# Attention and gated feed-forward on one core: the second tile's first weight columns put ahead of the first tile's second columns

## Chip, cores and metric

The kernel runs on one core of one Trainium2 chip. The metric is the device time of one execution in microseconds (us). The engines are TensorE (PE, with its weight loads PEld), VectorE (DVE), ScalarE (ACT), GpSimd (POOL) and SyncE (SP), which here issues most of the loads.

## What is computed

Causal attention with a decay for each head (no softmax), and after it a feed-forward block whose two up projections are multiplied with each other. All is in float32.

```python
def _attn_ref(q, k, v):                     # B, H, S, D = 8, 8, 576, 64
    scores = scale * np.matmul(q, k.transpose(0, 1, 3, 2))
    gamma = 1.0 - 2.0 ** (-5.0 - np.arange(H, dtype=np.float32))
    Dmat = np.where(rel >= 0, gamma[:, None, None] ** rel[None, :, :], 0.0)
    return np.matmul(scores * Dmat[None, :, :, :], v)

def _moe_ref(x, w1, w2, w3, w_out):         # x 4608x512, w1 and w2 512x1024, w3 1024x1024, w_out 1024x512
    a = x @ w1
    b = x @ w2
    h = a * b @ w3
    return h @ w_out
```

The weights arrive as float64; the kernel makes float32 of them from their bits.

## The kernel before

**Attention in units.** The batches are taken in four pairs, and the 576 positions of a pair in five chunks (64, then four of 128). A pair and a chunk make a unit; units 0 to 4 are the first pair. For a unit g, `load(g, ...)` issues the loads of k, q and v on SP's queue (L93). `scale(g, "q", True)` multiplies q by its decay on ACT, one instruction for each of eight heads (L202); `scale(g, "v", ...)` does the same for v. `front(g, names)` transposes k or q on PE into two PSUM banks (L218) and copies each bank to SBUF on ACT (L221). `score(g)` makes the score products on PE (L233) and multiplies them by the mask on DVE, four instructions (L236). `state(g)` adds k and v into the running state on PE (L255) and copies it on ACT (L259). `pv(g)` multiplies state and masked scores with q and v on PE (L274, L299); the function that it returns copies the result on ACT into the transposed tokens xT (L306).

**Tokens in tiles.** A pair has three tiles of 192 positions for each of its two batches, called (pair, n). Tile (0,0) is complete after unit 2, tile (0,1) after unit 3, and tile (0,2) after unit 4. `strassen_tokens(i, n, engine)` makes the four sums over a tile's quarters that the products need (L496).

**Up steps.** w1 and w2 are cut into four groups of 256 columns each. `up(i, n, fp, conv)` multiplies tile (i, n) with group fp of both weights by Strassen's scheme of seven products (Winograd's form), in a fixed order, each 8 matmuls (L528). `plus` adds a finished product on DVE to another part of the tile `c` (L533); it then runs `conv` steps of the weight conversion and one piece of work that was set aside in the list `aside`. Product p1 is copied to c by ACT twice (L546, L561), and at the end DVE multiplies the two halves of c into `ab` (L566). There is one buffer for c. Product S4 x B22, the last, is added onto the bank p5 after p5 has been read by the third `plus`.

**Weight conversion.** The weights come in blocks (0 to 3 make group 0, then four to a group), each loaded into one of five raw buffers (L342, L345). `conversion()` is a generator, and `convert(n)` runs n steps of it. To begin a block takes two steps: three ACT instructions for the exponents (L395 to L397; for block 7 L393 and L397) with DVE's L399, and DVE's L402. To end it takes two more: DVE's L413, and L426, which also calls for the next load. The exponents have two buffers. After the last block of a group three more steps make that group's weight sums S3, S2, and S1 with S4 (L149). `live["S", fp]` tells that they are issued; an up step needs them and calls for missing ones itself.

**Order.** The schedule is manual: each engine gets its instructions in the order in which the Python code issues them. From unit 3 on this order is written out by hand (L771 to L814): after `state(3)` the code converts until the sums of group 1 are issued, then come the scores of unit 3, the up step of tile (0,0) with group 1, the front of unit 4 (k and q), the output of unit 3, the token sums of tile (0,1), the scores of unit 4, the up step of tile (0,1) with group 0, the output of unit 4, and the up step of tile (0,1) with group 1. The number in `owed` is a count of conversion steps that the next up step runs after its first copy.

```python
def plus(ps, to, sb):
    nc.vector.tensor_add(c[:, to], ps, c[:, sb])
    convert(conv.pop(0) if isinstance(conv, list) else conv)
    for extra in (aside, spread):
        if extra:
            extra.pop(0)()
```

The first up step, `up(0, 0, 0, ..., first=True)`, has the list `aside` filled with: the scaling of q of unit 2 (run by the up step itself), an empty piece, the scaling of v of unit 2 on DVE, the front of k and the front of q of unit 2. Its `conv` is [0, 0, 2, 2, 2].

Of the kernel before, what the change touches and what calls it, by code (L numbers as in the profile page):

```python
# [19 lines left out]
def kernel(  # L20
# [13 lines left out]
    nc = tc.nc  # L34
# [160 lines left out]
    def scale(g, nm, scalar=False, engine=nc.gpsimd):  # L195
        c = g % NC
        sz = sizes[c]
        t, gam = live[nm, g], {"q": gq, "v": gk}[nm]
        t = t[:sz].rearrange("p (b h) d -> p b h d", b=2)
        if scalar:  # L200
            for h in range(H) if scalar is True else scalar:
                nc.scalar.mul(t[:, :, h, :], t[:, :, h, :], gam[:sz, c, h:h + 1])  # L202
            return
        engine.tensor_tensor(
            out=t, in0=t, in1=gam[:sz, c].unsqueeze(1).unsqueeze(3).to_broadcast([sz, 2, H, D]), op=ALU.mult)

    def front(g, names="kq"):
        c = g % NC
        sz = sizes[c]
        for nm in names:  # L210
            src = live[nm, g]
            dst = pools["fr"].tile([P, 2, NP, P], F32, tag=nm + "T", name=nm + "T",
                                   bufs=1 if nm == "k" and g >= NC else 2)
            for b in range(2):
                tp = acc.tile([P, NP, P], F32, tag="acc", name="tp")
                for p in range(NP):
                    h = b * H + 2 * p
                    nc.tensor.transpose(tp[:, p, :sz],  # L218
                                        src[:sz, h:h + 2, :].rearrange("p a d -> p (a d)"),
                                        ident[:sz, :sz])  # L220
                nc.scalar.copy(dst[:, b, :, :sz], tp[:, :, :sz])  # L221
            live[nm + "T", g] = dst

    def score(g):
        c = g % NC
        sz = sizes[c]
        kT, qT = live["kT", g], live["qT", g]
        pm = pools["fr"].tile([P, 2, 2, NP, P], F32, tag="pm", name="pm", bufs=1)
        for b in range(2):
            sc = [acc.tile([P, NP, P], F32, tag="acc", name="sc") for j in range(2)]  # L230
            for p in range(NP):
                for j, hs in enumerate(heads):
                    nc.tensor.matmul(sc[j][:sz, p, :sz], kT[hs, b, p, :sz], qT[hs, b, p, :sz],  # L233
                                     start=True, stop=True)
            for j in range(2):
                nc.vector.tensor_mul(pm[:sz, b, j, :, :sz], sc[j][:sz, :, :sz],  # L236
                                     mask[:sz, :sz].unsqueeze(1).to_broadcast([sz, NP, sz]))
        live["pm", g] = pm

    def state(g):  # L240
        c = g % NC
        sz = sizes[c]
        if c == NC - 1:
            return
        vs = live["v", g]
        kn = live["k", g]
        if c == 0:
            live["st"] = st_ps.tile([P, 2, NP, D], F32, tag="st", name="st")
        st = live["st"]

        for b in range(2):
            for p in range(NP):
                for j, hs in enumerate(heads):
                    h = b * H + 2 * p + j
                    nc.tensor.matmul(st[hs, b, p, :], kn[:sz, h, :], vs[:sz, h, :],  # L255
                                     start=(c == 0 and b == 0 and p == 0), stop=(c == NC - 2),
                                     skip_group_check=True)
        sb = pools["fr"].tile([P, 2, NP, D], F32, tag="sb", name="sb")
        nc.scalar.copy(sb, st)  # L259
        live["sb", g + 1] = sb  # L260
# [17 lines left out]
    def pv(g):  # L278

        if ("xps", g) not in live:  # L280
            pv_state(g)
        i, c = divmod(g, NC)
        sz = sizes[c]
        live["x", g] = True
        vs, pm, banks = live["v", g], live["pm", g], live["xps", g]

        parts = []
        for n in range(NB):
            lo, hi = max(starts[c], n * TB), min(starts[c] + sz, (n + 1) * TB)
            if lo < hi:  # L290
                m = i * NB + n
                if ("xT", m) not in live:
                    live["xT", m] = xps[m % 4 == 3].tile([P, NP, 2, TB], F32, tag="xT", name="xT")
                parts.append((live["xT", m], lo - n * TB, lo - starts[c], hi - lo))
        for m, (b, n) in enumerate(bank_order):
            for r in range(2):
                for half in range(2):
                    p, j = 2 * r + n, half ^ r
                    nc.tensor.matmul(banks[r][heads[half], b, n, :sz], vs[:sz, b * H + 2 * p + j, :],  # L299
                                     pm[:sz, b, j, p, :sz], start=(c == 0 and m == 0), stop=True,  # L300
                                     skip_group_check=True)

        def evict():
            for x, to, fr, n in parts:
                for r in range(2):
                    nc.scalar.copy(  # L306
                        x[:, 2 * r:2 * r + 2, :, to:to + n].rearrange("p n b s -> p b n s"),
                        banks[r][:, :, :, fr:fr + n])

        return evict  # L310
# [152 lines left out]
    def convert(n):  # L463

        for _ in range(n):
            if go_on() is not None:
                return
# [43 lines left out]
    def up(i, n, fp, conv=0, tail=True, first=False):  # L511
        m = every.index((i, n))
        while ("S", fp) not in live:
            assert go_on() is None
        if ("B", i, n) not in live:
            list(strassen_tokens(i, n))
        if fp == 0:
            live["ab", i, n] = (pools["ab3"] if m == 2 else ffn).tile([P, 2 * KF, TB], F32, tag="ab", name="ab")
        ab = live["ab", i, n]

        def product(ps, a, b):
            a, b = A(fp, a), live["B", i, n][b]
            new = ps is None
            if new:
                ps = acc.tile([P, 2, TB], F32, tag="acc", name="up")
            for w in range(2):
                for r in range(2):
                    nc.tensor.matmul(ps[:, w, :], a[:, w, r, :], b[:, r, :], start=(new and w == r == 0),  # L528
                                     stop=(w == r == 1), skip_group_check=True)
            return ps  # L530

        def plus(ps, to, sb):
            nc.vector.tensor_add(c[:, to], ps, c[:, sb])  # L533
            convert(conv.pop(0) if isinstance(conv, list) else conv)
            for extra in (aside, spread):
                if extra:
                    extra.pop(0)()


        sums = ()  # L540
        if fp == NQ - 1 and m < NB - 1 and has_x(*every[m + 1]) and ("B", *every[m + 1]) not in live:
            sums = strassen_tokens(*every[m + 1], nc.vector, True)
            aside.extend([lambda: next(sums)] * 4)
        c = ffn.tile([P, 4, 2, TB], F32, tag="c", name="c", bufs=1)
        p1 = product(None, "A11", "B11")
        nc.scalar.copy(c[:, 0], p1)  # L546

        convert(owed.pop() if owed else 0)
        if first:

            p7 = product(None, "S3", "T3")
            product(p1, "A12", "B21")
            aside.pop(0)()
        plus(product(None, "S2", "T2"), 1, 0)
        plus(p7 if first else product(None, "S3", "T3"), 2, 1)
        p5 = product(None, "S1", "T1")
        plus(p5, 3, 2)
        plus(product(None, "A22", "-T4"), 2, 2)
        if not first:
            product(p1, "A12", "B21")  # L560
        nc.scalar.copy(c[:, 0], p1)  # L561
        product(p5, "S4", "B22")
        plus(p5, 1, 1)

        list(sums)
        nc.vector.tensor_mul(ab[:, 4 * fp:4 * fp + 4, :], c[:, :, 0, :], c[:, :, 1, :])  # L566
        if tail:
            convert(conv)
# [224 lines left out]
    copies()  # L793
    load(4, "v")
    state(3)
    while ("S", 1) not in live:
        convert(1)
    score(3)
    aside.append(lambda: scale(4, "q", True))
    up(0, 0, 1, conv=2, tail=False)  # L800
    owed.append(2)
    front(4)
    convert(1)
    pv(3)()
    list(strassen_tokens(0, 1, nc.vector))
    score(4)
    aside.append(lambda: scale(4, "v", True))
    up(0, 1, 0, conv=2, tail=False)
    owed.append(2)
    pv(4)()  # L810
    up(0, 1, 1, conv=[2, 1, 0, 2, 2], tail=False)
    owed.append(2)
    up(0, 0, 2, conv=[2, 1, 1, 2, 2], tail=False)
# [509 lines left out]
```

## Time and profile before

| | us |
|---|---|
| median of 3 runs (lowest to highest) | 831.22 (830.67 to 832.04) |
| the profiled execution | 832.77 |
| its span, first to last instruction | 831.0 |
| granted TensorE clock, mean | 0.999 |

Where the first 100 us go on PE, ACT and DVE (busy us in each stretch of 10 us):

| stretch | PE | DVE | ACT | DMA share |
|---|---|---|---|---|
| 30 to 40 | 9.03 | 8.84 | 7.67 | 1.07 |
| 40 to 50 | 9.41 | 9.66 | 8.72 | 0.99 |
| 50 to 60 | 8.59 | 9.35 | 8.53 | 1.09 |
| 60 to 70 | 9.96 | 8.40 | 7.14 | 0.94 |
| 70 to 80 | 9.53 | 9.79 | 7.52 | 0.20 |
| 80 to 90 | 10.00 | 9.29 | 6.02 | 0.38 |

A row tells how long an engine was at work in that stretch; 10 means all the time. The change lies between 35 and 93 us. In a line of the timeline the first two figures are start and length in us, then come engine, line, operation and operands, the count of merged instructions, and in brackets the engine's idle time before it with what ended it.

### The profile page before, as it was taken

How to read it: one execution, taken by the hardware profiler on the slowest of the kernel's cores; microseconds unless marked ns; L12 is line 12 of the kernel's file. 1: busy time of each engine (PE TensorE's matmuls, PEld its weight loads, DVE VectorE, ACT ScalarE, POOL GpSimd, SP SyncE). 2: the span in 40 equal slices, each digit the busy share in tenths (PEclk: the TensorE clock that was granted, in tenths of full speed). 3: DMA queues.
4: the chain of work that ended last, by engine and by line, in shares of the span. 5: the costliest groups of instructions: out<-in, count | busy, mean ns of one | idle time of the engine just before them, and what ended most of it. 6: DMA issues, size and time to landing. Idle time of an engine off the chain costs nothing.

```text
span 831.0 us, 15815 instructions
## 1 busy us (share of the span) xinstructions
PE 817.5 (98%) x6117; PEld 737.0 (89%) x6117; DVE 547.6 (66%) x962; ACT 291.8 (35%) x609; POOL 222.3 (27%) x258
## 2 busy tenths in 40 slices
PE   8999999999999999999999999999999999999998
PEld 8889999744888998889999889998889998899987
DVE  4899999993544568754657755677745667646653
ACT  4787556572021111255443024341034331033300
POOL 1000000001303332125547015565006460045600
PEclk9999999999999999999999999999999999999999
DMA  9995454446237665988786347978245453146401
GB/s 191 226 224 137 79 131 134 117 126 104 99 66 195 113 151 186 266 264 206 200 228 184 92 88 209 240 224 217 56 92 180 163 191 114 36 149 214 141 26 51
DMA packets 196812, 126.96 MB, mean 153 GB/s; under 512 B 157848, under 2 KB 178456, under 8 KB 196736
## 3 DMA queue, kind: packets, MB, share of 16 engines
q1 hardware_dynamic: 168560, 50.40, 29.6%
q0 software_dynamic: 12480, 65.67, 24.3%
q10 hardware_dynamic: 15696, 9.87, 4.5%
q8 instruction: 48, 0.79, 0.4%
q14 instruction: 28, 0.23, 0.1%
HBM read 103.62 MB, written 22.28 MB: 152 GB/s over the span
## 4 chain that ended last, share of the span: by engine, by line
PE 89%; DVE 6%; DMA 2%; issue 1%; SPq 1%; ACT 1%; ACTq 0%; POOL 0%; DVEq 0%; POOLq 0%
PE po L651 24%; PE up L1060 17%; PE up L528 14%; PE seed L1060 13%; PE ps L477 7%; PE xps L299 3%; PE sc L233 3%; PE xps L274 2%; PE tp L218 2%; PE st L255 1%; SPq L171 1%; DVE pm L236 1%; DVE ab L1032 1%; PE idle L131 1%; DMA ld_v<-in_v_dram 1%
## 5 line engine op out<-in xcount | busy, mean ns | idle before, releaser
L651 PE MATMUL po<-w3o,ab 128*128 128x256 f32 x552 | 125.0, 381 | 2.3 <-DVE ot L655 1.0
L651 PEld LDWEIGHTS po<-w3o,ab 128*128 128x128 f32 x552 | 103.7, 190 | 18.9 <-DVE ot L655 2.5
L1065 POOL TENSOR_TENSOR cc<-cc 128x384 f32<-128x384 f32 x112 | 109.3, 1002 | 3.8 <-ACT cc L1083 2.4
L1072 DVE TENSOR_TENSOR cc<-seed,cc 128x384 f32<-128x384 f32 x88 | 48.7, 553 | 69.0 <-PE seed L1060 59.3
L181 POOL TENSOR_TENSOR bl_q<-bl_q,gqs 128x512 f32<-128x512 f32 (+1 forms) x26 | 26.0, 1020 | 185.8 <-DMA bl_q<-in_q_dram 182.3
L1060 PE MATMUL up<-xT,ra 128*128 128x192 f32 x384 | 73.7, 328 | 0.1
L528 PE MATMUL up<-xT,wA 128*128 128x192 f32 x384 | 70.7, 328 | 1.0 <-DVE xT L496 1.0
L236 DVE TENSOR_TENSOR pm<-sc,mask 128x512 f32<-128x512 f32 (+1 forms) x80 | 45.4, 627 | 35.1 <-PE sc L233 35.1
L1072 DVE TENSOR_TENSOR cc<-up,cc 128x384 f32<-128x384 f32 x88 | 48.5, 551 | 30.2 <-PE up L1060 21.8
L533 DVE TENSOR_TENSOR c<-up,c 128x384 f32<-128x384 f32 x80 | 44.1, 552 | 36.7 <-PE up L528 35.7
L651 PE MATMUL po<-wB,forms 128*128 128x256 f32 x288 | 65.4, 379 | 0.7 <-DVE pm L236 0.7
L528 PEld LDWEIGHTS up<-xT,wA 128*128 128x128 f32 x384 | 63.3, 190 | 2.4 <-PE up L528 1.2
L1060 PEld LDWEIGHTS up<-xT,ra 128*128 128x128 f32 x384 | 63.7, 190 | 1.4 <-DMA ra<-kept 0.4
L961 POOL DMA_DIRECT2D ra<-kept x54 | 30.5, 565 | 118.7 <-PE seed L1060 93.8
L651 PEld LDWEIGHTS po<-wB,forms 128*128 128x128 f32 x288 | 54.6, 190 | 8.4 <-DVE pm L236 1.1
L1079 ACT COPY seed<-up 128x384 f32<-128x384 f32 x56 | 25.9, 463 | 100.2 <-PE up L1060 56.6
L477 PE MATMUL ps<-wo,w3T 128*128 128x512 f32 x128 | 55.1, 592 | 0.0
L1060 PE MATMUL up<-ra 128*128 128x192 f32 x288 | 54.7, 326 | 0.0
L477 PEld LDWEIGHTS ps<-wo,w3T 128*128 128x128 f32 x128 | 24.3, 190 | 30.1 <-issue 29.7
L1060 PE MATMUL seed<-e,ra 128*128 128x192 f32 x256 | 50.9, 329 | 0.0
L1060 PEld LDWEIGHTS up<-ra 128*128 128x128 f32 x288 | 48.1, 190 | 0.1
L528 PE MATMUL up<-T,wS 128*128 128x192 f32 x256 | 46.7, 326 | 1.4 <-DVE wS L149 1.4
(134 smaller groups left out, 1479.1 us busy)
## 6 DMA issues: line engine op xcount, KB each, us to landing
ra<-kept POOLq DMA_DIRECT2D x54, 896.0 KB, 4.9
raw<-in_moe_w_dram SPq DMA_DIRECT2D x72, 128.0 KB, 3.0
bl_q<-in_q_dram SPq DMA_DIRECT2D x192, 32.0 KB, 3.3
out_dram<-ot ACTq DMA_DIRECT2D x41, 128.0 KB, 2.3
bl_k<-in_k_dram SPq DMA_DIRECT2D x136, 32.0 KB, 3.5
raw<-in_moe_w_dram SPq DMA_DIRECT2D x16, 256.0 KB, 5.4
ld_k<-in_k_dram SPq DMA_DIRECT2D x8, 512.0 KB, 6.1
raw<-in_moe_w_out_dram SPq DMA_DIRECT2D x32, 128.0 KB, 2.8
```

What stands on the lines that cost most here:

```text
L181: nc.gpsimd.tensor_tensor(out=part, in0=part, in1=gqs[:, :, n0:n0 + n].unsqueeze(3).to_broadcast([P, NP, n, BL]), op=ALU.mult)
L233: nc.tensor.matmul(sc[j][:sz, p, :sz], kT[hs, b, p, :sz], qT[hs, b, p, :sz], start=True, stop=True)
L236: nc.vector.tensor_mul(pm[:sz, b, j, :, :sz], sc[j][:sz, :, :sz], mask[:sz, :sz].unsqueeze(1).to_broadcast([sz, NP, sz]))
L477: nc.tensor.matmul(ps, live["w3T", ft][:, g, :], live["wo"][:, g, :], start=(g == 0), stop=(g == KF - 1))
L528: nc.tensor.matmul(ps[:, w, :], a[:, w, r, :], b[:, r, :], start=(new and w == r == 0), stop=(w == r == 1), skip_group_check=True)
L533: nc.vector.tensor_add(c[:, to], ps, c[:, sb])
L651: nc.tensor.matmul(ps[nm], a[A][:, f, :], live["W"][B][:, f, :], start=(f == 0 and not on), stop=(f == NP - 1), skip_group_check=True)
L961: engine.dma_start(ring[n % 3], kept[n % 14 // 7][nm])
L1060: nc.tensor.matmul(ps[:, w, :], weight_of(slot, a, w), B[b], start=(new and w == 0), stop=True, skip_group_check=True)
L1065: nc.gpsimd.tensor_tensor(out=o, in0=o, in1=i, op=ALU.add)
L1072: nc.vector.tensor_add(c[:, j], ps, with_add[:, j])
L1079: nc.scalar.copy(p6, p1)
```

## The change

Two things are edited. In the first up step, `plus` runs the piece of set-aside work before the conversion steps and not after them; other up steps are as they were. And the hand-written order after `state(3)` becomes: scores of unit 3; scaling of q and front of k of unit 4; output of unit 3; token sums of tile (0,1); front of q of unit 4; one conversion step; scores of unit 4; the up step of tile (0,1) with group 0, with three conversion steps in each `plus` in place of two; output of unit 4; conversion until the sums of group 1 are issued; the up step of tile (0,0) with group 1; the up step of tile (0,1) with group 1 as before. The scaling of q of unit 4 is issued directly, and no longer as a set-aside piece of an up step.

```diff
         def plus(ps, to, sb):
             nc.vector.tensor_add(c[:, to], ps, c[:, sb])
+            if first and aside:
+                aside.pop(0)()
             convert(conv.pop(0) if isinstance(conv, list) else conv)
-            for extra in (aside, spread):
+            for extra in (spread,) if first else (aside, spread):
                 if extra:
                     extra.pop(0)()
...
     state(3)
+    score(3)
+    scale(4, "q", True)
+    front(4, "k")
+    pv(3)()
+    list(strassen_tokens(0, 1, nc.vector))
+    front(4, "q")
+    convert(1)
+    score(4)
+    aside.append(lambda: scale(4, "v", True))
+    up(0, 1, 0, conv=3, tail=False)
+    pv(4)()
     while ("S", 1) not in live:
         convert(1)
-    score(3)
-    aside.append(lambda: scale(4, "q", True))
     up(0, 0, 1, conv=2, tail=False)
     owed.append(2)
-    front(4)
-    convert(1)
-    pv(3)()
-    list(strassen_tokens(0, 1, nc.vector))
-    score(4)
-    aside.append(lambda: scale(4, "v", True))
-    up(0, 1, 0, conv=2, tail=False)
-    owed.append(2)
-    pv(4)()
     up(0, 1, 1, conv=[2, 1, 0, 2, 2], tail=False)
     owed.append(2)
```

## Prediction

> **What bounds the kernel now.** I read the page first, then busy time by stretches, then who TensorE (PE) waited for, then the timeline around the change, then the landing times of the loads in it.
>
> ```profile
> PE 817.5 (98%) x6117; PEld 737.0 (89%) x6117; DVE 547.6 (66%) x962; ACT 291.8 (35%) x609; POOL 222.3 (27%) x258
> ```
>
> The whole-kernel shares say TensorE. By stretches (length, busy PE, PEld, DVE, ACT, POOL, clock, DMA share, GB/s):
>
> ```profile
> 49.70:92.70 43.00, 41.04 (x409) 39.00 (x410) 38.97 (x69) 30.48 (x60) 0.00 (x0) 1.00 0.63 149
> 92.70:157.00 64.30, 64.27 (x392) 63.36 (x392) 61.93 (x110) 38.89 (x59) 0.00 (x0) 1.00 0.52 123
> 157.00:212.50 55.50, 55.50 (x134) 24.89 (x133) 35.15 (x53) 26.27 (x38) 4.01 (x4) 1.00 0.50 109
> ```
>
> The moved steps lie in the first row. PE idles 1.96 us there, which is all that a better order can win. From 92.70 PE has no hole, so a delay handed on there stays to the end. VectorE (DVE) is busy 62 of 64 us: it has no room either. The holes by cause (us, times, longest):
>
> ```profile
> PE up L528 <- DVE wS L149: 1.4, 1, 1.4
> ...
> PE st L255 <- DVE ld_v L204: 0.6, 1, 0.6
> PE up L528 <- DVE c L533: 0.5, 1, 0.5
> ```
>
> The 1.4 is the first tile's second up step waiting for weight sums, at 55.79. Around it (start, length, engine, line):
>
> ```profile
> 45.83 5.16 SPq L93 DMA_DIRECT2D ld_q<-in_q_dram  x1
> ...
> 50.82 2.06 PE L233 MATMUL sc<-qT,kT 64*128 64x128 f32 x32
> ...
> 51.72 0.69 DVE L402 SCALAR_TENSOR_TENSOR m<-raw,m 128x512 f32<-128x512 uint32 x1
> ...
> 55.79 1.54 PE L528 MATMUL up<-T,wS 128*128 128x192 f32 x8 [1.41 <-DVE wS L149]
> ...
> 56.88 2.48 DVE L236 TENSOR_TENSOR pm<-sc,mask 128x512 f32<-128x512 f32 x4
> 56.98 2.43 ACT L202 ACTIVATE ld_q<-ld_q,gq 128x128 f32<-128x128 f32 x8
> ```
>
> The first line is the load of the fifth unit's q. Its landing (last figure, us from issue):
>
> ```profile
> ld_q<-in_q_dram SPq DMA_DIRECT2D x1, 512.0 KB, 10.9
> ```
>
> So it lands at 45.83 + 10.9 = 56.7, and its scaling by ScalarE (ACT) ran from 56.98. The same front end later:
>
> ```profile
> 67.88 1.10 ACT L221 COPY qT<-tp 128x512 f32<-128x512 f32 x2
> 68.54 2.06 PE L233 MATMUL sc<-qT,kT 64*128 64x128 f32 x32
> 68.83 1.24 ACT L306 COPY xT<-xps 128x256 f32<-128x256 f32 x4
> 69.55 0.56 DVE L496 TENSOR_TENSOR xT<-xT 128x384 f32<-128x384 f32 x1 [0.94 <-ACT xT L306]
> ...
> 70.52 1.57 PE L528 MATMUL up<-xT,wA 128*128 128x192 f32 x8
> ```
>
> What follows calls units and weight blocks by their numbers, and writes up(t,f) for the up step of tile t of the first pair with weight group f; durations in sums are taken from start to start.
>
> **The change, part by part.** *(a) In the first up step, the set-aside work is issued ahead of the conversion steps.* No instruction is added. On ACT the kT copies of unit 2 (37.23, 1.07) pass block 4's exponents (35.02 to 37.31), the qT copies pass block 5's. kT cannot start before its transposes (36.59 plus about 0.6), so it keeps 37.23; block 4 takes block 5's slot (38.19), qT stays at 40.41, and block 5 (2.3) now stands ahead of the copy of c at L561: 43.7 instead of 41.35. The product at L566 needs that copy, so it goes from 42.94 to 44.15, and DVE behind it (mask products of unit 2, block 6, scaling of v3) shifts by 1.2; ACT likewise. PE follows by about 1.2 at the third unit's transposes. On the final time I price this at 0, because the wait in (b) covers it: with the shift, the mask products of unit 3 end at 56.1 and its output matmuls at about 58, still before the q that (b) waits for. Without that cover it costs 1.2.
>
> *(b) score(3), scaling of q4, front of unit 4, pv(3), token sums, score(4) come before up(0,1), which gives way to up(1,0).* Before, up(0,1), 7 products x 1.30 = 9.1 us of PE, hid the landing of q4, its scaling and the fronts. Now nothing does. ACT takes them as written: scaling 56.75 to 59.15 (2.43), kT copies to 60.2 (1.07), xT copies of pv(3) to 61.35 (1.24), qT copies from 61.3, the first half done at 61.85 (0.53). PE runs dry at about 58, does the q transposes as heads arrive, and starts score(4) at 61.9; 1.97 later, at 63.9, up(1,0) starts. In the trace of before the same work plus up(0,1) was done at 70.52. Loss: 63.9 + 9.15 - 70.52 = **+2.5**. The removed 1.41 and 0.6 are already inside this difference. Queued behind the waiting scaling on ACT: kT, xT, qT; behind xT on DVE: the token sums, block 7's end, the mask products. DVE ends L402 at 52.41 and the mask products of unit 3, now next, at 54.9 (2.48), or 56.1 with (a); then it stands still until the first two xT copies are done, at 60.85 (0.72 after their start, as at 68.83 and 69.55): 4.8 us of an engine that has no slack.
>
> *(c) up(1,0) with 3 conversion steps per sum instead of 2.* DVE: token sums 60.85 to 62.98 (2.13), L413 of block 7 (0.61), mask products to 66.0 (2.4), first sum at 66.8, when PE's second product ends. Then L426, S3, S2, S1, S4 (0.61+0.70+0.72+0.61+0.61), second sum (0.47), L399, L402 (1.05), third sum ends 72.6. PE's last product adds onto the bank that the third sum reads; it is ready at 63.9 + 7.91 = 71.8 and starts at 72.65. That 0.85 replaces the 0.47 at 79.06; from start to last product 8.75 against 8.54: **+0.2**. pv(4) follows with no wait, up(0,1) starts 4.43 later (79.06 to 83.49 in the trace): 77.1.
>
> *(d) up(0,1), now here.* The fifteenth step of (c) puts block 11's exponents (2.3) on ACT. They need one of two buffers, freed by block 9's L426 at 78.25, and end at 80.55; xT copies of unit 4 (1.08) and the copy at L546 (0.5) stand behind them, so c is ready at 82.05. DVE finished L566 at 79.45: another 2.6 idle. Sum 0.47, L402, L413 (1.2), sum 0.47, L426, L399 (1.05), third sum ends 85.8; PE is ready for its last product at 77.1 + 7.91 = 85.0. **+0.85**, and up(1,1) starts at 87.15 (83.49 before).
>
> *(e) up(1,1), unmoved.* DVE arrives late: fourth and fifth sums with L426, S3, S2, S1, S4 end at 91.1, L566 at 92, two owed steps 93.0, then sum, L413, L426, sum, L399, sum to 96.15; PE is ready at 95.05. **+1.1.** up(0,2) then starts at about 97.4 against 92.70, and its own third sum (100.1 + 4.5 = 104.4) is before PE's 105.3. One conversion step fewer in all (26 against 27 here) is caught up later and costs nothing: w3's third transposed tile is ready at 163.8 (L430, 162.59 + 1.25) and wanted at 171 (157.2 plus two tiles of 55.1/8). Loads: the SP queue gets the same transfers; those of blocks 12 to 15 come up to 11 us later, but with over 5 us before their exponents.
>
> **Sum:** 2.5 + 0.2 + 0.85 + 1.1 = +4.65. The profiled execution took 832.77, its span 831.0, with 1.8 outside the span; the sum makes it 837.4. Against the median of 831.22, which I use: **835.9**.
>
> **Unknown prices.** The landing: DMA was at its limit there, so the SP queue shifts little; 0.5 us earlier or later moves (b) by 0.5. The waits (c) to (e) come from adding some 40 DVE and ACT rows: between 0 (then +2.5 less the 0.47 that goes, 833.2) and 1.5 more than I have. (a) between 0 and 1.2.
>
> The clock in all rows above is 1.00, with no PE hole longer than 1.4; the new hole is some 3 us with eight transposes in it, and I price it at 0. The Trainium skill (TensorE: Matmul & The Clock Gate, Why this matters for your kernels) says that gaps over about 3 us between bursts bring the clock back to half, and Part 4 of it that transposes do not count as busy. By that, an estimate, a half-speed window of 3.4 us would add 1.7, and the time would be 837.6; no trace here shows such a gap.
>
> **Rivals.** *Overlap wins (faster).* up(1,0) needs no second columns, so PE works while DVE makes their sums, and the 1.41 + 0.47 go: 829.3. The place is score(4). It decides if up(1,0) starts 4.65 earlier than 63.9, at 59.2, thus q4 landing by 52.0, 6.2 after its issue; if (c) to (e) vanish with it, 54.2 is enough. The measured 10.9 and 2.43 speak against. 5%.
>
> *Only the hole at score(4).* DVE catches up in (c) to (e) because the sums are hidden by free banks: 833.2. For it: before, DVE recovered its lag by 86.47. Against: the third sum must be read before PE's last product, whatever banks are free. 22%.
>
> *More than the sum.* (a) isn't covered, 1.2, or the waits (c) to (e) are the full 1.5 larger, or both: 837.1 to 838.6. 10%.
>
> *Nothing changes.* A later stage takes the delay in, 831.2. Against: PE 64.27 of 64.30 and 55.50 of 55.50. 6%.
>
> **Numbers.** My forecast has 57%. Its own range is 834.3 to 837.2; the range to hold 8 in 10 goes down to the second rival and up past (a): 832.7 to 837.8. A change of 0.2% (1.7 us) is about what a measurement here can tell from none. Faster by that 0.05, within it 0.07 (nothing changes, and the low edge of the second rival), slower 0.88.
>
> **What will show it.** In the new trace: scaling of q4 on ACT at about 56.7 behind the DMA; score(4) at about 62, up(1,0) at 64; DVE idle before the token sums 4 to 6 us; a wait of the first sum of up(0,1) on ACT's L546; three waits of PE on c L533 near 1 us each; up(0,2) at 97.4; equal spacing after it. Score(4) before 60, or a PE without those three waits, would prove me wrong.

## The result, and the profile after

The changed kernel took 837.83 us in the median (835.52 to 840.66, 6 runs), the kernel before 831.34 (830.67 to 833.33, 6 runs). The ratio is 1.0075, 95% interval 1.0052 to 1.0098: slower by 6.5 us where 4.7 were forecast. The forecast was 835.9, with 832.7 to 837.8 as its range; the median lies at the upper end of it. The interval means 4.3 to 8.1 us more, so the times alone do not set the forecast's 4.7 apart from the 6.5. The profiled execution of the changed kernel took 839.02, its span 837.3 (before 832.77 and 831.0): 6.3 more in the spans, and these 6.3 are accounted for here.

The busy line of the page, after the change:

```profile
PE 820.6 (98%) x6117; PEld 738.5 (88%) x6117; DVE 548.2 (65%) x962; ACT 291.2 (35%) x609; POOL 222.0 (27%) x258
```

The share of TensorE is 98% as before: the loss doesn't show there. Busy time by stretches does show it (length, PE, PEld, DVE, ACT, POOL, clock, DMA share, GB/s). The first stretch holds the same work as 49.70 to 92.70 before, up to the start of up(0,2):

```profile
49.60:98.64 49.04, 43.79 (x412) 40.51 (x410) 39.24 (x69) 30.65 (x61) 0.00 (x0) 0.97 0.52 128
98.64:163.00 64.36, 64.33 (x393) 63.53 (x393) 61.96 (x111) 38.37 (x58) 0.00 (x0) 1.00 0.53 123
163.00:218.50 55.50, 55.50 (x134) 24.89 (x133) 35.94 (x55) 27.11 (x40) 3.78 (x4) 1.00 0.51 110
```

It is 6.04 longer (49.04 against 43.00), and up(0,2) starts 5.94 later, at 98.64 instead of 92.70. PE idles 5.25 us in it where it idled 1.96, and PE's own busy time grew by 2.75 though its work is the same: 1.6 of that is score(4) and the first product after it, the rest is nearly all in the transposes (L218, 2.94 instead of 1.91), which now run as the heads of q4 arrive. The clock column is new: 0.97 instead of 1.00. The next two stretches are as long as before, so nothing was given back.

Who PE waited for (us, times, longest), the two rows that grew:

```profile
PE up L528 <- DVE c L533: 2.3, 3, 0.9
PE sc L233 <- ACT qT L221: 2.0, 2, 1.8
```

The wait for weight sums is gone, 1.4 us. In its place stand 1.8 for the transposed q of unit 4 and three waits for sums of c. The chain that ended last (start, length, what) goes through the first of them:

```profile
45.56 10.81 DMA ld_q<-in_q_dram
56.39 2.45 ACT ld_q L202 x8
58.84 0.95 ACT kT L221 x2
59.79 1.08 ACT xT L306 x4
60.87 0.50 ACT qT L221
61.41 3.40 PE sc L233 x32
```

Load of q4, scaling, kT copies, xT copies, qT copies, score(4): the queue that the prediction wrote down, in its order. The timeline of the rows around it, with what each engine waited for in brackets:

```profile
60.35 0.56 DVE L496 TENSOR_TENSOR xT<-xT 128x384 f32<-128x384 f32 x1 [4.52 <-ACT xT L306]
...
61.41 3.40 PE L233 MATMUL sc<-qT,kT 64*128 64x128 f32 x32 [1.75 <-ACT qT L221]
...
64.74 1.81 PE L528 MATMUL up<-xT,wA 128*128 128x192 f32 x8
...
73.82 1.57 PE L528 MATMUL up<-xT,wS 128*128 128x192 f32 x8 [0.77 <-DVE c L533]
...
83.18 0.56 DVE L533 TENSOR_TENSOR c<-up,c 128x384 f32<-128x384 f32 x1 [2.37 <-ACT c L548]
...
86.98 1.57 PE L528 MATMUL up<-xT,wS 128*128 128x192 f32 x8 [0.66 <-DVE c L533]
...
97.23 1.57 PE L528 MATMUL up<-xT,wS 128*128 128x192 f32 x8 [0.89 <-DVE c L533]
...
98.64 1.46 PE L528 MATMUL up<-xT,wA 128*128 128x192 f32 x8
```

DVE stands still for 4.52 ahead of the token sums, and for 2.37 ahead of the first sum of up(0,1), behind ACT's copy (L546 before, two lines lower now). What the sum did not have is the length of score(4): 3.40 for 32 matmuls that took 2.06 before. The stretches of 2 us around it:

```profile
58.00:60.00 2.00, 1.32 (x8) 0.67 (x6) 0.00 (x0) 2.00 (x7) 0.00 (x0) 1.00 1.26 262
60.00:62.00 2.00, 0.59 (x8) 0.59 (x10) 1.58 (x3) 1.84 (x6) 0.00 (x0) 0.96 1.00 210
62.00:64.00 2.00, 2.00 (x24) 2.00 (x22) 2.00 (x5) 0.00 (x0) 0.00 (x0) 0.50 0.45 103
64.00:66.00 2.00, 2.00 (x14) 1.78 (x13) 1.58 (x3) 0.00 (x0) 0.00 (x0) 0.68 0.68 218
66.00:68.00 2.00, 2.00 (x14) 2.00 (x13) 0.16 (x2) 1.41 (x5) 0.00 (x0) 1.00 0.16 52
```

PE worked 1.9 of the 4 us ahead of 62. Then its clock was granted at 0.50, from about 61.9 to 65.3. Score(4) and the first product of up(1,0) ran in that time: 3.33 from start to start instead of 1.98, and 1.65 instead of 1.41, so 1.6 us.

### The profile page after: what moved, and what is told of

It reads as the page before. It is cut to its first block, busy times and chain, and to the rows that moved or that the text cites. A ratio compares the mean times of both kernels' runs of the same rounds, so it can differ in the third digit from the quotient of the medians.

```text
span 837.3 us, 15813 instructions
## 1 busy us (share of the span) xinstructions
PE 820.6 (98%) x6117; PEld 738.5 (88%) x6117; DVE 548.2 (65%) x962; ACT 291.2 (35%) x609; POOL 222.0 (27%) x258
## 4 chain that ended last, share of the span: by engine, by line
PE 82%; DVE 7%; DMA 4%; issue 3%; ACT 2%; SPq 1%; POOL 1%; ACTq 0%; DVEq 0%; POOLq 0%
PE po L653 24%; PE up L1062 16%; PE seed L1062 12%; PE up L528 12%; PE ps L477 7%; PE sc L233 3%; PE xps L299 3%; PE xps L274 1%; DMA ld_q<-in_q_dram 1%; PE st L255 1%; PE tp L218 1%; SPq L171 1%; DMA ra<-kept 1%; DVE ab L1034 1%; DVE c L533 1%
## 5 line engine op out<-in xcount | busy, mean ns | idle before, releaser
L653 PE MATMUL po<-w3o,ab 128*128 128x256 f32 x552 | 124.9, 381 | 2.3 <-DVE ot L657 1.0
L653 PEld LDWEIGHTS po<-w3o,ab 128*128 128x128 f32 x552 | 103.7, 190 | 18.8 <-DVE ot L657 2.5
L653 PE MATMUL po<-wB,forms 128*128 128x256 f32 x288 | 65.4, 379 | 0.3 <-DVE pm L236 0.3
L653 PEld LDWEIGHTS po<-wB,forms 128*128 128x128 f32 x288 | 54.6, 190 | 8.1 <-DVE pm L236 0.7
```

The lines of the kernel that those rows point to most:

```text
L653: nc.tensor.matmul(ps[nm], a[A][:, f, :], live["W"][B][:, f, :], start=(f == 0 and not on), stop=(f == NP - 1), skip_group_check=True)
```

## The experiments

My theory after the result: PE is held at score(4) by ACT's queue behind q4; the hole lets the clock fall; and DVE, stopped ahead of the token sums and again behind ACT's exponents, makes three later products wait. Rivals: the first edit is to blame; or the early landing of q4 alone would make the change win; or DVE's lateness is a matter of ACT's queue only. "1.0069 (1.0057 to 1.0081)" is a ratio to the kernel before on the same chip, with its 95% interval. The kernel before took 832.3 to 832.4 there.

**The changed kernel once more.**

> The changed kernel itself, beside the next three on one chip. Its loss against the kernel before should again be 0.5 to 1.0%, and its times should spread by several us, since the fall of the clock depends on where its 3.41 us windows lie: with the clock falling for one window, for two, or not at all.

839.51, ratio 1.0085 (1.0069 to 1.0101), 837.67 to 841.43. In the profiled execution score(4) took 3.78, and the clock stayed at 0.50 for two windows, 6.83 us, as expected of some executions: from the start of score(4) to the second product of up(1,0) it is 6.24 us, against 4.98 in the first profile and 3.39 before. The loss is there again.

**Filler matmuls in the hole.** `keep_busy(n)`, which the kernel has already, multiplies the identity n times with itself on PE; nobody reads the result.

```diff
     list(strassen_tokens(0, 1, nc.vector))
+    keep_busy(3)
     front(4, "q")
+    keep_busy(7)
     convert(1)
     score(4)
```

> The changed kernel with filler matmuls on PE: three ahead of the q transposes of unit 4 and seven behind them, so that PE has work while it waits for score(4). Theory (the clock fell to 0.50 from 61.9 to 65.3 because PE ran dry at 58): the clock stays at 1.00, score(4) takes 2.0 instead of 3.40 and the first product 1.55 instead of 1.81, the time falls by about 1.6 to 836.2, and the runs lie closer together. Rival (the clock is not moved by the idle time, or the lost time is hidden by DVE being late anyway): no change, 837.8.

```profile
59.55 1.73 PE L131 MATMUL idle<-ident 128*128 128x128 f32 x14
...
61.45 2.06 PE L233 MATMUL sc<-qT,kT 64*128 64x128 f32 x32 [0.18 <-ACT qT L221]
```

With PE kept at work the clock stayed at 1.00 (0.999 or 1.000 in the mean of all five executions), score(4) took 2.06, and up(1,0) started at 63.44 instead of 64.74. That the idle time moves the clock is shown. What it is worth in time isn't: 837.87, ratio 1.0069 (1.0057 to 1.0081), against 1.0075 and 1.0085 with overlapping intervals, where 836.2 was expected. Its five times lie within 1.9 us, those of the changed kernel within 5.1 and 3.8; since the kernel before itself spread by 2.9 over the 11 runs beside this one and by 4.0 over 18 others, this proves little. In the profile up(0,2) starts 1.53 earlier than in the changed kernel, but 0.9 of that is lost after it, in waits of PE for DVE at L653 and L1064 that are longer in this execution by about 1; whether that is chance is open.

**The new order without the first edit.** (`plus` as before the change.)

```diff
-            if first and aside:
-                aside.pop(0)()
             convert(conv.pop(0) if isinstance(conv, list) else conv)
-            for extra in (spread,) if first else (aside, spread):
+            for extra in (aside, spread):
```

> The changed kernel without its first edit: the first up step converts ahead of the set-aside work, as before. Theory (the 1.2 us by which that edit delays DVE is covered by the wait for q4 on ACT): mask products of unit 3 end about 1.2 earlier, score(4) starts within 0.3 of 61.4, the time stays at 837.8 within 0.7. Rival (the first edit's delay is handed on): 836.6, and score(4) starts near 60.2.

838.43, ratio 1.0075 (1.0061 to 1.0089). The mask products of unit 3 start at 52.15 instead of 53.36, as expected 1.2 earlier, and score(4) starts at 61.66. The first edit costs nothing in the new order, since the wait for q4 covers it. The rival that blames it falls.

**The first edit alone, on the kernel before.** (The same two lines, put in.)

> The kernel before with the first edit alone (set-aside work ahead of the conversion steps in the first up step). Theory (without the wait for q4 that covers it, its delay of DVE by 1.2 reaches PE, since the second up step waits for weight sums that DVE makes in order): the wait of 1.41 at 55.79 grows to about 2.6, the time to 832.5. Rival (it is hidden on PE): 831.3.

```profile
55.60 1.54 PE L528 MATMUL up<-T,wS 128*128 128x192 f32 x8 [1.41 <-DVE wS L149]
```

833.19 against 832.42, ratio 1.0005 (0.9992 to 1.0017): between 0.7 us gained and 1.4 lost, which holds both theories. The profile says more. From score(2) to the second product of up(0,1) it is 15.87 us (39.73 to 55.60), before 14.76 (41.03 to 55.79): the delay of 1.1 is there and reaches PE. It doesn't come as a longer wait for the weight sums, as I had expected; that stays at 1.41, because PE itself is late, after waits for mask products (0.44, before none) and for v3 (0.85, before 0.59). In this execution the opening was 1.3 earlier, which hides it in the span.

**Block 11's exponents after the first copy of up(0,1).**

```diff
-    up(0, 1, 0, conv=3, tail=False)
+    up(0, 1, 0, conv=[3, 3, 3, 3, 2], tail=False)
+    owed.append(1)
     pv(4)()
```

> The changed kernel, with the last conversion step of up(1,0) (it begins block 11) run after the first copy of up(0,1) instead. Theory (block 11's exponents on ACT stand ahead of the copy at L548, which the next sum of DVE waits for): that copy moves from 82.66 to about 80.5, DVE's wait of 2.37 there goes nearly to 0, PE's waits for c in up(0,1) and up(1,1), 0.66 and 0.89, go to below 0.3 each, the time falls by about 1.3 to 836.5. Rival (DVE is late from its stop ahead of the token sums, whatever ACT does): the waits stay, 837.8.

```profile
81.32 0.48 ACT L548 COPY c<-up 128x384 f32<-128x384 f32 x1 [0.26 <-DVE ab L568]
...
82.11 0.56 DVE L533 TENSOR_TENSOR c<-up,c 128x384 f32<-128x384 f32 x1 [0.54 <-PE up L528]
```

The copy now waits for `ab` and no longer for the exponents, and DVE's 2.37 became 0.54, spent on PE. PE's last products in up(0,1) and up(1,1) show no wait; the one in up(1,0), 0.77, stays. 837.22, ratio 1.0051 (1.0037 to 1.0065), against 1.0075 and 1.0085 of the changed kernel: 0.24 to 0.34% less, where 0.16% was expected, though the clock was low for 6.83 us in its profile. So ACT's three instructions did cause two of the three waits.

**Four conversion steps in DVE's stop.**

```diff
     pv(3)()
+    convert(4)
     list(strassen_tokens(0, 1, nc.vector))
     front(4, "q")
-    convert(1)
     score(4)
     aside.append(lambda: scale(4, "v", True))
-    up(0, 1, 0, conv=3, tail=False)
+    up(0, 1, 0, conv=[3, 3, 2, 2, 2], tail=False)
```

> The changed kernel with four conversion steps (the end of block 7 and the sums of group 1, 3.3 us of DVE) ahead of the token sums of tile (0,1), where DVE stands still for 4.5 us, and fewer in up(1,0), the same in all. Theory (DVE's stop ahead of the token sums is what makes its sums late later): PE's waits for c in up(1,0), up(0,1) and up(1,1), 0.77, 0.66 and 0.89, go to below 0.2 each; 2.2 less than the changed kernel; score(4) still starts at 61.4 and the clock still falls. Rival (only the ACT exponents of block 11 matter, as e4 moved them): the first wait stays, at most 1.5 less.

All of PE's waits in this stretch, 49 to 100 us:

```profile
PE sc L233 <- ACT qT L221: 1.8, 1, 1.8
PE st L255 <- DVE ld_v L204: 0.8, 1, 0.8
PE tp L218 <- ACT ld_q L202: 0.5, 2, 0.3
```

All three waits for c are gone, the first too. Score(4) starts at 61.37 and takes 3.66. 835.71, ratio 1.0047 (1.0030 to 1.0064), against 839.51 of the changed kernel on the same chip: 3.8 less, 2.2 were expected. A part of the 3.8 is the clock's: among executions with the same mean clock, 0.998, it is 835.59 and 835.78 against 837.67 and 838.52, 2.4 less. Block 11's exponents come earlier by themselves, at 76.20 instead of 79.51, because DVE frees their buffer earlier (L426 at 75.26 instead of 78.78), and no longer hold up the copy of c. So the lateness of DVE explains all three waits; moving ACT's exponents was another way to give a part of it back.

The length of the stop is not what counts. In the runs that keep ACT's order and leave the conversion behind the stop, DVE's idle time ahead of the token sums goes from 3.98 us (the load of q4 first, below) to 6.34 (the changed kernel once more), and the first wait for c is 0.77 in all of them. What counts is the 3.3 us of conversion that come after the stop and not in it.

**The same, with the filler matmuls.** (Both edits.)

> As the second kernel of this group, with the filler matmuls of the first experiment. Theory (clock and DVE's lateness are separate terms): no fall of the clock, score(4) in 2.06, 1.5 less than the second kernel in the middle and a narrower spread, leaving the wait of score(4) itself, +2 to +2.5 against the kernel before. Rival (filling does not pay, as the first experiment's time, 837.87, seems to say): the same time as the second kernel.

Score(4) takes 2.06 and the clock holds through it; up(0,2) starts at 94.76 instead of 95.63. 835.42, ratio 1.0038 (1.0024 to 1.0051), 0.3 less than without filler where 1.5 was expected. As in the first experiment, the profile shows the gain at its place and the times don't confirm its size; by the times alone the rival, that filling does not pay, stands.

**q4 scaled by DVE.**

```diff
-    scale(4, "q", True)
+    scale(4, "q", engine=nc.vector)
```

> The changed kernel with q4 scaled by one DVE instruction (1.22) instead of eight on ACT (2.45); DVE stands idle there. Theory (ACT's queue behind the scaling sets score(4)): kT copies at 55.3, scaling 56.4 to 57.6, q transposes follow the output matmuls of unit 3 with no hole, xT copies at 58, qT at 59.1, score(4) at about 59.6 instead of 61.4; the hole is too short for the clock to fall (score(4) in 2.06); 1.8 + 1.5 less, 834.5. Rival (the landing of q4 alone sets it, or DVE's late sums eat the gain): 836.5 or more.

```profile
59.84 2.06 PE L233 MATMUL sc<-qT,kT 64*128 64x128 f32 x32 [0.24 <-ACT qT L221]
```

834.9, ratio 1.0037 (1.0022 to 1.0051), as expected. Score(2) began as in the changed kernel (40.95 and 40.93), score(4) 1.6 earlier, and the clock did not fall (1.000 in the mean of all five executions); the three waits for c stay (0.77, 0.67, 0.89). ACT's queue is the second half of what holds score(4).

**The load of q4 first.**

```diff
-        if n >= 4:
+        if n >= 4 and n != 4:
             load_block()
...
-    load(4, "kq")
+    load(4, "qk")
+    load_block()
     front(3, "k")
```

> The changed kernel with the load of q4 issued ahead of that of k4 and of weight block 8. Theory (the landing pins the scaling, and ACT is next): q4 lands near 52.5, the scaling starts when ACT is free, at 55.3 instead of 56.39, score(4) at about 60.3, the time falls by 1.1, or by up to 2.6 if the hole gets too short for the clock to fall: 835.2 to 836.7. Rival of the prediction (an early q4 is enough for the overlap to win): below 831.3. Other rival (ACT or k4, now later, sets it anyway): 837.8.

835.6, ratio 1.0039 (1.0024 to 1.0054). Score(4) at 59.38 in 2.06; in this execution the opening was 1.5 earlier too (score(3) at 50.34 instead of 51.85), and since the scaling now begins when ACT is free, at 53.71, it profits from that; the 2.0 are not the load's alone. The waits for c stay. The prediction's rival, that an early q4 makes the overlap win, falls: q4 landed at 44.45 + 6.9 = 51.35, inside the 52.0 that the rival asked for, but up(1,0) started at 61.36 and not at 59.2, since ACT's queue stands between, and the kernel is still 0.24 to 0.54% slower than before.

**Both: q4 first, and four conversion steps in DVE's stop.**

> The changed kernel with both: the load of q4 first, and four conversion steps ahead of the token sums. Theory (the loss is the wait of score(4), the fall of the clock that follows it, and DVE's lateness, and nothing else): score(4) at 59.4 in 2.06, no waits for c above 0.2, up(0,2) at 92.7 as before the change, the time within 0.1% of the kernel before. Rival (something else is lost, too): slower than before by 0.2% or more.

Its waits of PE in the same stretch:

```profile
PE tp L218 <- DMA ld_k<-in_k_dram: 1.2, 1, 1.2
PE st L255 <- DVE ld_v L204: 0.8, 1, 0.8
PE sc L233 <- ACT qT L221: 0.5, 1, 0.5
```

832.37, and the kernel before 832.37; ratio 1.0005 (0.9995 to 1.0015). Clock 1.00, no wait for c, up(0,2) at 91.79. Counted from score(2), which began 1.65 earlier in this execution, that is 52.4 us, before the change 51.7. So the terms of the theory are the loss, but for at most 0.15%: with the wait for q4 shortened, the clock kept and DVE's stop used, the new order is about as fast as the old one, and not faster.

**Several mends at once.** The new order without the first edit, q4 scaled on DVE, its transposes and copies ahead of those of unit 3's output, block 11 later; the four conversion steps are not put into DVE's stop. (A part of the edit, against the changed kernel.)

```diff
-    scale(4, "q", True)
+    scale(4, "q", engine=nc.vector)
     front(4, "k")
-    pv(3)()
-    list(strassen_tokens(0, 1, nc.vector))
+    evict = pv(3)
     front(4, "q")
+    evict()
+    list(strassen_tokens(0, 1, nc.vector))
     convert(1)
```

> The changed order without its first edit, with q4 scaled on DVE, its transposes and copies ahead of the copies of unit 3's output, and block 11 begun after the first copy of up(0,1). Theory (these are all the terms of the loss): score(4) at about 59, up(1,0) at 61, up(1,1) at 82.7 to 83.5 against 83.49 before; 830.5 to 831.5, no more than the 1 us that the hole of before was worth. Rival (DVE stays late, having stopped ahead of the token sums): 833 or more.

```profile
71.48 2.58 PE L528 MATMUL up<-xT,wS 128*128 128x192 f32 x8 [1.95 <-DVE c L533]
```

834.69, ratio 1.0026 (1.0010 to 1.0042). Here I was wrong. Score(4) came at 59.49, as expected, but DVE's stop was still there: DVE ran four steps of block 7 and its sums in up(1,0), and the last product waited 1.95 for c, long enough for the clock to fall behind it (0.50 from 72 on). The token sums started at 60.51, no earlier than in the changed kernel (60.35), because the copies of xT now stand behind those of q; so a PE that is 1.9 earlier met the same late DVE. Where both came earlier together, as with q4 scaled by DVE (58.78 and 59.84), the wait stayed at 0.77.

**The kernel before, with its hole filled.** A piece of work from the list `beside` is run after the first copy of an up step, and this is the k transposes of unit 4.

```diff
         convert(owed.pop() if owed else 0)
+        if beside:
+            beside.pop(0)()
...
+    beside.append(lambda: front(4, "k"))
     up(0, 0, 1, conv=2, tail=False)
     owed.append(2)
-    front(4)
+    front(4, "q")
```

> The kernel before with the k transposes of unit 4 moved into PE's hole of 1.41 in up(0,1), after its first product; their copies on ACT (1.07) then stand ahead of block 8's exponents and of the scaling of q4. Theory (k4 lands at 53.7, the hole is at 54.4 to 55.8): the hole shrinks by about 1.0 and the transposes are gone from 63.66: 830.4. Rival (a PSUM bank or ACT holds the second product back): 831.3 or more.

```profile
54.18 1.04 PE L218 MATMUL tp<-ident,ld_k 128*128 128x128 f32 x8
55.76 1.54 PE L528 MATMUL up<-T,wS 128*128 128x192 f32 x8 [0.54 <-DVE wS L149]
57.59 1.57 PE L528 MATMUL up<-xT,wA 128*128 128x192 f32 x8 [0.30 <-DVE pm L236]
```

831.89 against 832.42, ratio 0.9988 (0.9977 to 0.9999). The hole of 1.41 shrank to 0.54, a bank held by scores costs 0.30, and up(0,2) starts at 91.83, with score(2) at 41.01 as before (41.03). It is faster than the kernel before by 0.01 to 0.23%; the step that fits the hole is a small one whose data are there, and not a whole up step.

## Why the prediction was right, and where it was off

| step of the prediction | forecast | in the profile |
|---|---|---|
| (a) first edit, in the new order | 0 | 0 (838.43 without it) |
| (b) landing of q4 | 56.7 | 45.56 + 10.8 = 56.4 |
| (b) score(4), start | 61.9 | 61.41 |
| clock in the hole at score(4) | 1.00, price 0 | 0.50 for about 3.4 us, 1.6 |
| (b) up(1,0), start | 63.9 | 64.74; 63.4 without the fall |
| (c) last product of up(1,0), late by | 0.85 | 0.93 (idle 0.77) |
| (d) DVE waits for ACT's copy | 2.6 | 2.37 |
| (d) last product of up(0,1), late by | 0.85 | 0.82 (idle 0.66) |
| (e) last product of up(1,1), late by | 1.1 | 1.04 (idle 0.89) |
| up(0,2), start | 97.4 | 98.64 |
| spans, after less before | 4.65 | 6.3 |

The prediction counts from start to start, and the lateness above is counted so: a product's row lasts 1.46 us while the next begins 1.30 after it, so the idle time of PE is about 0.16 less.

The mechanism was right in each of its steps, and the direction with it. One reading was not: the wait of 0.6 for v3 (L204), which (b) seems to mean where it calls 0.6 removed, is not touched by the change and stands in the new trace at 0.85; the sum doesn't use it. The term that was mis-sized is the clock. The prediction said of the new hole "some 3 us with eight transposes in it, and I price it at 0", on the ground that no row showed a fall. The longest hole shown was 1.4 us, so those rows couldn't speak for a longer one. The Trainium skill (TensorE: Matmul & The Clock Gate, Why this matters for your kernels) was set against it there, and the estimate of 1.7 that the prediction worked out from it gave 837.6; the profile shows 1.6 and the runs 837.83. Its price was the better guide. Where rows end short of the case and a page goes on, its price belonged into the sum.

The page's limit, gaps over about 3 us, is another matter, and there the traces differ from it. PE was never idle for over 1.75 us at a stretch ahead of the fall (3.55 if the transposes are taken as idle), and in the run of several mends a single wait of 1.95 was enough. Nor do the traces bear out that transposes don't count: in the run with q4 first PE was busy 2.12 us of 3.41 from 52.51 on, 1.07 of them with transposes, and the clock held; 1.47 us without a transpose, in the run of several mends, didn't hold it.

With 1.6 for the clock the sum is 4.65 + 1.6 = 6.25, against 6.3 in the spans. That the sums agree so well is partly chance. Counted as the prediction counts, (b) cost 2.02 without the fall (63.39 + 9.15 - 70.52; 2.5 forecast), (c) 0.30 (0.2), (d) 0.99 (0.85), (e) 1.04 (1.1), the clock 1.59 and the stretch behind up(0,2) some 0.35, which wasn't forecast. So (b), 0.5 too dear, made up for what (c), (d) and the end had too little.

Of the rivals, "only the hole at score(4)" falls by the three waits. "Overlap wins" falls twice: q4 came at 56.4, and with an early q4 the kernel was still slower (ratio 1.0039). "Nothing changes" falls by the stretches behind up(0,2), which are as long as before. "More than the sum" was the one that came closest in time, for another reason than it gave. What the prediction said of DVE, an engine that has no slack, is what the experiments bear out: with four steps of work in DVE's stop, all waits for c were gone.

Open is what a fall of one window costs in the median. In the profile it is 1.6 us at its place. The pairs with and without filler differ by 0.3 us (835.71 and 835.42) and by 0.0 or 1.6 (837.83 or 839.51, and 837.87 with filler, from three groups of runs), with intervals that overlap. The second window does show: the mean clock of every execution is on record, and of the changed kernel's twelve the four with 0.996, the value of the profile with two windows, took 839.30 to 841.43, and the six with 0.998, the value of the profile with one, 835.52 to 839.02; that is 2.7 us in the mean. Only one execution had 1.000, and it took 836.55.

## What to carry to other kernels

A step moved ahead to fill a hole takes its cover with it: ask first what it was hiding, here 9.1 us over a load, its scaling and two fronts, and where in each engine's written order the next wait then falls. On an engine with no slack, work that is left behind a stop is paid for later, at whatever reads its results, so fill the stop with work that is due anyway, or leave the order. And a hole on TensorE that is longer than any in the trace needs a price for the clock too.

## What the runs showed of the hardware

The clock fell and rose on a grid. In the clock records of all profiles here, the falls inside the kernel begin 10.24, 47.79, 54.61 or 58.03 us after the record's start (which in the changed kernel is 14.07 us into the span), which are 3, 14, 16 and 17 times 3.413, and last 3.41 or 6.83. After the first 40 us, each fall follows a window of that grid in which PE was busy for 0.34 to 0.57 of the time (1.40 of 3.41 us in the changed kernel, 1.47 in the run of several mends), and windows with 0.59 or more are followed by none (2.00 of 3.41 us, from 52.87 on, in the kernel before with the first edit). The hole of 1.41 before the change brought no fall, nor did those of 0.77 to 0.89. In the first 25 us this border doesn't hold: three falls follow windows with 0.61 to 0.71, and none follows one with 0.55 (from 17.97 on, q4 first and four steps in the stop); why is open. The falls after 40 us lasted two windows in the two profiles in which PE began its work 0.6 and 0.8 us after the clock had fallen, and one in those in which it began with the fall or up to 0.5 before. So what a hole costs depends on where it lies on that grid, and differs between executions of one kernel.

The opening, up to score(2), took 39.4 to 41.3 us, while q4's landing did not follow: its scaling began at 56.39, 56.44 and 56.35 in three kernels whose score(2) began at 40.93, 39.59 and 40.78, and at 57.19 in the changed kernel's second profile, with score(2) at 39.92. Here the load, queued behind others, landed by its queue's time and not by that of the engines that wanted it. So where the opening differs, two profiles are best compared from one shared instruction to another.
